# The up products of a SwiGLU block, re-formed as two nested levels of a seven-product scheme, on one Trainium2 core

## The chip, the cores and the metric

The kernel runs on one core of one Trainium2 chip. The metric is the device time of one execution in microseconds (us). Before the change it is 1042.5 us, the median of three runs (1040.97 to 1045.37). The core's engines have separate instruction queues: TensorE (PE) with its weight loads (PEld), VectorE (DVE), ScalarE (ACT), GpSimd (POOL) and SyncE (SP). DMA transfers are issued mainly by SP, the stores of one stage by ACT.

## The reference

Everything is float32. Eight batches of eight heads (576 positions of 64 values) go through a retention layer; its output, 4608 tokens of 512 values, goes through a SwiGLU block with 1536 hidden columns.

```python
scores = (1 / sqrt(64)) * q @ k.transpose(0, 1, 3, 2)
ret = scores * Dmat            # gamma_h ** (i - j) for i >= j, else 0
attn = ret @ v                 # (8, 8, 576, 64)
x = attn.transpose(0, 2, 1, 3).reshape(4608, 512)
g = x @ w_gate                 # (512, 1536)
silu = g * (1.0 / (1.0 + exp(-g)))
out = (silu * (x @ w_val)) @ w_out      # (1536, 512)
```

## The kernel before

**Stages.** The tokens are cut into a first tile of 512 and four tiles of 1024 (`n` = 1 to 4). Stage 0 makes the first tile with plain products, while the weights are being unpacked. Each later tile has an *up stage* (hidden values) and then a *down stage* (outputs). The retention layer is done in *ticks*, one for each batch and pair of heads: small matmuls on PE and pieces of work on DVE and ACT that are dealt out between the products (`part_on`). Each tick also loads the q, k and v of a later pair; this *head load* is 12 or 13 small DMAs on SP's queue (`load`, L306 to L317) and follows the transposes of the tick on DVE (L516), whose buffer it fills again. `merge` spreads ticks evenly over the products of a stage. Ticks stand in the up stages of tiles 1 and 2, in the down stages of tiles 1 and 2, and a few that have no load any more stand in tile 3.

**The up products before.** An up stage has three parts (`qd`), each giving 512 hidden columns of gate and of value. In one part the weights are 4 column blocks of 128 by 2 halves of the 512 inputs, and the tokens are 4 blocks of 256. The table `UP` writes out a scheme of 26 products for this, in place of the usual 32. A product has four matmuls (gate and value, two slices of 128 inputs; L1124), each with 128x128 weights and 256 columns. The line of a product in `UP` says which of four PSUM banks it adds to, which sum of x blocks it reads (made on DVE and POOL, L910), which sum of weight blocks (made on POOL in tile 1, L910 and L1095), and how the bank is then read: copies on ACT (L1058), sums with the bank on DVE (L1061), sums without it on POOL, and at last SiLU on ACT (L1145) and the gate-times-value product on DVE or POOL (L1148 to L1152).

**Weight operands.** In tile 1 the weights are in SBUF. Each operand (a block or a sum) is stored to DRAM once it has been used (`up_ops`, L1128, from ACT's queue, 256 KB). In tiles 2 to 4 the operands come back by DMA on SP's queue (`fetch`, L1022) to a ring of eight places: when product m is done, the fetch for product m + 8 is issued. The down stage uses the same ring (384 KB each). For the first down stage, eight fetches are issued in the last steps of tile 1's up stage. The order on each queue is the order of the program; nothing is reordered.

**After a product.** A bank is taken by the product whose line begins it and may be taken again once its last read is done. The list `rested` keeps the four banks in the order of their use.

Of the kernel before, what the change touches and what calls it, by code (L numbers as in the profile page):

```python
# [22 lines left out]
def tables(gamma, scale, L):  # L23
# [27 lines left out]
UP = [  # L51
    "0= | 8: sub 8 2 6, sub 9 0 8, sub 10 4 9 | 8: neg 8 6, sub 9 2 6, sub 10 3 7, add 11 1 10 | copy 0, copy 1",
    "1= | 10: sub 11 3 8, sub 12 7 11 | 3: nad 12 3 6 | copy 2, copy 3",
    "2= | 0:  | 9:  | copy 4, copy 5",
    "3= | 12:  | 11: sub 8 11 6 | copy 6",
    "0+ | 9:  | 12: add 9 2 3 | sub 2 b 2, sub 4 4 2, out 4 4",
    "1= | 4: sub 13 0 2 | 10: nad 11 11 0 | add 2 b 2, neg 12 2",
    "3+ | 11: add 14 4 12 | 8:  | add 1 b 1",
    "0+ | 13: sub 15 14 0 | 9: add 12 4 5, add 10 2 12, nad 8 7 10 | sub 5 5 b, out 6 5",
    "1+ | 14: sub 16 0 1, add 17 5 16 | 11:  | add 6 b 6",  # L60
    "3= | 15: sub 18 4 6, sub 19 5 18 | 0: add 6 6 7 | add 7 b 6, neg 0 7",
    "2+ | 17:  | 8: sub 9 3 0 | copy 4",
    "0= | 19: add 20 7 10 | 5: add 11 0 2 | copy 5",
    "1= | 6:  | 6: add 7 7 5 | sub 0 b 0, out 14 0",
    "3+ | 20: sub 21 4 17 | 9: add 8 5 6 | sub 3 b 3",
    "2= | 3: sub 22 16 6 | 11: add 0 0 1 | add 7 b 3, out 7 7",
    "0+ | 21: add 18 18 7 | 7: nad 9 1 3 | add 2 b 2, sub 4 4 2, add 5 5 4",
    "1+ | 22:  | 8: sub 11 1 10 | add 2 b 2, neg 13 2",
    "3= | 18: sub 23 1 3, sub 24 5 23 | 0: nad 6 6 12 | add 6 b 6",
    "0= | 7:  | 9: add 2 2 4 | add 1 b 1, add 3 b 3, neg 15 1, neg 3 3, add 6 6 3, neg 2 6",  # L70
    "2+ | 24: sub 1 1 5 | 11: sub 12 0 12 | add 3 b 3",
    "1+ | 16:  | 6:  | sub 4 b 4",
    "3= | 1: sub 2 16 2 | 2: sub 1 5 1 | sub 5 b 5, add 0 b 4, out 8 5, out 9 0",
    "2+ | 23: sub 25 7 24 | 12: nad 3 3 10 | add 7 b 4, out 1 7",
    "1+ | 2:  | 4:  | neg 10 b",
    "3+ | 25:  | 1:  | sub 3 b 3, out 11 3",
    "0= | 5:  | 3:  | add 4 b 4, neg 5 4",
]
# [55 lines left out]
]  # L134

# [20 lines left out]
def kernel(  # L156
# [739 lines left out]

    up, down = lines(UP), lines(DOWN)
    N = len(up)
# [13 lines left out]
    up_ops = [[dr.tile([P, 512], F32, name=f"up{qd}_{i}") for i in range(N)] for qd in range(NQ)]  # L912
# [85 lines left out]
    def up_view(qd):  # L998
        return lambda s: (w_up[:, qd, :, s // 2, s % 2, :] if s < 8
                          else extra[:, s - 8].rearrange("p (g x) -> p g x", g=2))  # L1000

    def x_view(n):
        return lambda s: (xs[n][:, 2 * (s // 4) : 2 * (s // 4) + 2, (s % 4) * TB : (s % 4 + 1) * TB] if s < 8
                          else xsum[s - 8].rearrange("p (c x) -> p c x", c=2))

# [4 lines left out]

    fetches = [("dn", 1, i) for i in range(N)]
    for n in range(2, NTILE):
        fetches += [("up", qd, i) for qd in range(NQ) for i in range(N)] + [("dn", n, i) for i in range(N)]
    fetched = [0]
    turn = [5, 4, 1, 6, 7, 2, 0, 3]

    def fetch():
        m = fetched[0]
        if m < len(fetches):
            what, a, i = fetches[m]  # L1020
            src = up_ops[a][i] if what == "up" else dn_ops[i]
            nc.sync.dma_start(out=ring[:, turn[m % 8], 0 : src.shape[-1]], in_=src)  # L1022
            fetched[0] += 1

    used = [0]

    def operand():
        m = used[0]
        used[0] += 1
        return ring[:, turn[m % 8]]  # L1030
# [15 lines left out]
    products = []  # L1046

    def reads(ops, bank, busy, result, spread=False):

        at = lambda a: bank if a == "b" else part[int(a)]  # L1050
        old = len(products)
        for op in ops:
            if op[0] in ("copy", "add", "sub"):
                while any(a == op[1] for a, _ in products):
                    products.pop(0)[1]()
                    old -= 1
            if op[0] == "copy":
                nc.scalar.copy(out=at(op[1]), in_=bank)  # L1058
            elif op[0] in ("add", "sub"):
                eng = nc.vector if "b" in op or (busy and not spread) else nc.gpsimd  # L1060
                eng.tensor_tensor(out=at(op[1]), in0=at(op[2]), in1=at(op[3]),  # L1061
                                  op=ALU.add if op[0] == "add" else ALU.subtract)
            else:
                product = result(int(op[1]), at(op[2]), op[0] == "neg", op[2] == "b" or busy)
                if product and op[2] == "b":
                    product()
                elif product:
                    products.append((op[2], product))
        for _ in range(old):
            products.pop(0)[1]()  # L1070


    x_ops = [op for line in up for op in line[3]]
    X_FIRST = 8

    def x_sums(n, lo, hi, vector):
        for op in x_ops[lo:hi]:
            add(nc.vector if vector or op[0] == "nad" else nc.gpsimd, op, x_view(n))

    def negated(qd, i):  # L1080

        view = up_view(qd)
        for op in up[i][5]:
            if op[0] == "nad":
                nc.scalar.mul(out=view(int(op[1])), in_=view(int(op[3] if op[3] == op[1] else op[2])), mul=-1.0)

    def w_sums(qd, i):
        view = up_view(qd)
        for op in up[i][5]:
            if op[0] == "nad":  # L1090

                dst, a, b = [view(int(s)) for s in op[1:]]
                if op[3] == op[1]:
                    a, b = b, a
                nc.gpsimd.tensor_tensor(out=dst, in0=dst, in1=b, op=ALU.subtract)  # L1095
            else:
                add(nc.gpsimd, op, view)

    def first_sums(qd, lo, hi):

        engines = [nc.scalar, nc.gpsimd, nc.vector, nc.gpsimd]
        for op, eng in list(zip(up[0][5], engines, strict=True))[lo:hi]:
            if op[0] == "neg":
                nc.scalar.mul(out=up_view(qd)(int(op[1])), in_=up_view(qd)(int(op[2])), mul=-1.0)
            else:
                add(eng, op, up_view(qd))

    def up_step(n, qd, i):
        label, opens, xslot, _, wslot, _, ops = up[i]
        busy = n == 1  # L1110
        if qd == 0:
            done = lambda i: X_FIRST + (min(3 * i, 2 * i + 2, i + 6) if busy else i)
            x_sums(n, done(i), done(i + 1), busy)
        if busy:
            if i > 1:
                w_sums(qd, i)
            w = up_view(qd)(wslot)
        else:
            w = operand()[:, 0:512].rearrange("p (g x) -> p g x", g=2)
        rhs = x_view(n)(xslot)  # L1120
        b = bank(label, i == 0)
        for gv in range(2):
            for c in range(2):
                m = nc.tensor.matmul(b[:, gv * TB : (gv + 1) * TB], w[:, gv, ts(c, P)], rhs[:, c, :],  # L1124
                                     start=(opens and gv == 0 and c == 0), stop=(c == 1), skip_group_check=True)
        stepped.append(m)
        if busy:
            nc.scalar.dma_start(out=up_ops[qd][i].rearrange("p (g x) -> p g x", g=2), in_=w)  # L1128
            if i in (20, 23) and qd + 1 < NQ:
                first_sums(qd + 1, *((0, 2) if i == 20 else (2, 4)))  # L1130
            if i == 24 and qd + 1 < NQ:
                negated(qd + 1, 1)
                w_sums(qd + 1, 1)
            if 0 < i < N - 1:
                negated(qd, i + 1)
            if qd + 1 == NQ:
                for _ in range({21: 3, 22: 2, N - 1: 3}.get(i, 0)):
                    fetch()
        else:
            fetch()  # L1140

        def result(o, src, negative, vector):
            s = io[:, (silus[0] % 4) * TB : (silus[0] % 4 + 1) * TB]
            silus[0] += 1
            nc.scalar.activation(out=s, in_=src[:, 0:TB], func=AF.Silu, scale=-1.0 if negative else 1.0)  # L1145
            dst = hid[:, qd, o // 4, o % 4]
            if negative:
                return lambda: nc.vector.scalar_tensor_tensor(out=dst, in0=src[:, TB : 2 * TB], scalar=-1.0, in1=s,  # L1148
                                                              op0=ALU.mult, op1=ALU.mult)
            if vector:  # L1150
                return lambda: nc.vector.tensor_tensor(out=dst, in0=src[:, TB : 2 * TB], in1=s, op=ALU.mult)
# [115 lines left out]
    for m, f in enumerate(down_order):  # L1267
# [5 lines left out]
        if m == 5:  # L1273
            first_sums(0, 0, 1)
# [71 lines left out]
```

## Time and profile before

| what | value |
|---|---|
| median of 3 runs | 1042.5 us |
| span of the profiled execution, first to last instruction | 1037.2 us |
| PE busy / PEld busy | 1023.1 us (99%) / 846.0 us (82%) |
| DVE / ACT / POOL busy | 633.2 (61%) / 299.6 (29%) / 419.9 us (40%) |
| up stage of tile 1 | 173.8 to 320.5 us |
| down stage of tile 1 | 320.5 to 400.3 us |
| up stages of tiles 2, 3, 4 | 400.3 to 545.5, 622.6 to 762.2, 831.4 to 966.0 us |
| DVE busy in the up stage of tile 1 / 2 / 3 / 4 | 105.1 / 76.1 / 68.0 / 56.9 us |
| POOL busy in the same | 96.6 / 49.7 / 51.4 / 49.6 us |

The page gives no separate time for the profiled execution; its span is 5.3 us below the median of the timed runs. Busy times say how much an engine had to do, not whether anybody waited for it. Waits are in the view of waits (who waited for whom) and in the view of instructions in order of time, which gives the start, the duration and, in square brackets, the idle time before an instruction and what ended it. [...]

### The profile page before, as it was taken

What the parts mean: (1) busy time and instruction counts of PE and PEld (TensorE: products, weight loads), DVE (VectorE), ACT (ScalarE), POOL (GpSimd) and SP (SyncE); (2) the same over time, 40 slices, a digit from 0 to 9 for tenths busy, and PEclk for the clock granted to TensorE, in tenths of its full rate; (3) what the DMA queues carried; (4) which work ended last, traced back from release to release, by engine and by line L of the source; (5) the groups of instructions that cost most, each with busy time, mean ns of one, the idle gap of its engine ahead of it and who ended that gap; (6) DMA issues with size and microseconds to landing.
All of it is one profiled execution on the core that took longest, in us unless ns stands there. A gap on an engine that the chain in (4) does not pass through costs nothing.

```text
span 1037.2 us, 21564 instructions
## 1 busy us (share of the span) xinstructions
PE 1023.1 (99%) x8440; PEld 846.0 (82%) x8440; DVE 633.2 (61%) x1070; ACT 299.6 (29%) x653; POOL 419.9 (40%) x369
## 2 busy tenths in 40 slices
PE   6999999999999999999999999999999999999998
PEld 5654555888888888888888888888888888888887
DVE  4488878676768667446458685435465644344644
ACT  3566433253544222222322103223211022231110
POOL 3401265867564236522134057222242583222425
PEclk9999999999999999999999999999999999999999
DMA  9999877777679887674686686555554465555653
GB/s 240 258 279 263 200 218 269 204 205 191 196 194 265 211 244 220 177 197 133 188 231 173 176 208 208 153 142 153 159 171 148 143 196 153 153 153 160 182 163 100
DMA packets 307244, 199.12 MB, mean 192 GB/s; under 512 B 215944, under 2 KB 251784, under 8 KB 307144
## 3 DMA queue, kind: packets, MB, share of 16 engines
q1 hardware_dynamic: 275720, 161.17, 58.2%
q10 hardware_dynamic: 30784, 36.18, 10.4%
q8 instruction: 67, 1.10, 0.5%
q0 software_dynamic: 640, 0.39, 0.2%
q14 instruction: 33, 0.27, 0.1%
HBM read 157.58 MB, written 40.11 MB: 191 GB/s over the span
## 4 chain that ended last, share of the span: by engine, by line
PE 93%; DMA 3%; DVE 1%; ACT 1%; issue 1%; SPq 1%; POOL 0%; DVEq 0%; ACTq 0%; POOLq 0%
PE bankC L1124 13%; PE bankE L1124 13%; PE bankB L1124 13%; PE bankA L1124 13%; PE bankB L1173 7%; PE bankC L1173 7%; PE bankE L1173 7%; PE bankA L1173 7%; PE outer L556 2%; PE bankA L877 2%; PE bankB L877 1%; PE bankE L877 1%; PE outer L583 1%; PE inner L597 1%; PE inner L567 1%; PE bankC L877 1%
## 5 line engine op out<-in xcount | busy, mean ns | idle before, releaser
L1061 POOL TENSOR_TENSOR rest<-rest 128x512 f32<-128x512 f32 x65 | 91.7, 1415 | 234.3 <-DVE rest L1061 212.8
L1145 ACT ACTIVATE io<-rest 128x256 f32<-128x256 f32 x180 | 75.0, 416 | 305.4 <-DVE rest L1061 262.4
L1124 PE MATMUL bankC<-rest,arena 128*128 128x256 f32 x544 | 129.0, 380 | 0.0
L1124 PE MATMUL bankA<-rest,arena 128*128 128x256 f32 x544 | 128.7, 379 | 0.0
L910 POOL TENSOR_TENSOR arena<-arena 128x512 f32<-128x512 f32 (+1 forms) x72 | 110.6, 1549 | 37.3 <-DMA up<-arena 26.5
L1124 PE MATMUL bankB<-rest,arena 128*128 128x256 f32 x512 | 121.2, 380 | 0.5 <-DMA arena<-up 0.5
L1124 PE MATMUL bankE<-rest,arena 128*128 128x256 f32 x512 | 121.4, 380 | 0.1
L1152 POOL TENSOR_TENSOR arena<-rest,io 128x256 f32<-128x256 f32 x72 | 51.9, 726 | 167.7 <-ACT io L1145 167.7
L1124 PEld LDWEIGHTS bankA<-rest,arena 128*128 128x128 f32 x544 | 103.2, 190 | 14.5 <-issue 0.5
L1124 PEld LDWEIGHTS bankC<-rest,arena 128*128 128x128 f32 x544 | 102.9, 190 | 14.4 <-POOL arena L910 0.3
L1124 PEld LDWEIGHTS bankB<-rest,arena 128*128 128x128 f32 x512 | 97.0, 190 | 14.0 <-issue 0.8
L1124 PEld LDWEIGHTS bankE<-rest,arena 128*128 128x128 f32 x512 | 97.0, 190 | 13.7 <-DVE rest L1061 0.5
L910 POOL TENSOR_TENSOR rest<-rest 128x256 f32<-128x256 f32 (+1 forms) x69 | 68.9, 1020 | 71.8 <-DMA dn<-rest 35.3
L1061 DVE TENSOR_TENSOR rest<-bankB,rest 128x512 f32<-128x512 f32 x72 | 48.9, 687 | 67.1 <-PE bankB L1124 52.5
L1061 DVE TENSOR_TENSOR rest<-bankC,rest 128x512 f32<-128x512 f32 x72 | 48.9, 687 | 65.5 <-PE bankC L1124 46.9
L1061 DVE TENSOR_TENSOR rest<-bankA,rest 128x512 f32<-128x512 f32 x72 | 48.9, 687 | 61.2 <-PE bankA L1124 45.1
L1061 DVE TENSOR_TENSOR rest<-bankE,rest 128x512 f32<-128x512 f32 x71 | 48.2, 687 | 60.5 <-PE bankE L1124 47.1
L1148 DVE SCALAR_TENSOR_TENSOR arena<-rest,io 128x256 f32<-128x256 f32 x84 | 56.7, 676 | 10.8 <-ACT io L1145 10.8
L1173 PE MATMUL bankC<-arena 128*128 128x256 f32 x252 | 58.3, 380 | 0.1
L1173 PE MATMUL bankB<-arena 128*128 128x256 f32 x252 | 58.2, 381 | 0.0
L1173 PE MATMUL bankA<-arena 128*128 128x256 f32 x252 | 57.9, 379 | 0.0
L1173 PE MATMUL bankE<-arena 128*128 128x256 f32 x252 | 57.9, 379 | 0.0
(204 smaller groups left out, 1626.1 us busy)
## 6 DMA issues: line engine op xcount, KB each, us to landing
arena<-up SPq DMA_DIRECT2D x234, 256.0 KB, 2.6
arena<-dn SPq DMA_DIRECT2D x104, 384.0 KB, 3.8
up<-arena ACTq DMA_DIRECT2D x78, 256.0 KB, 3.7
dn<-rest SPq DMA_DIRECT2D x78, 128.0 KB, 1.8
out_dram<-rest SPq DMA_DIRECT2D x31, 256.0 KB, 3.9
qk<-in_q_dram SPq DMA_DIRECT2D x108, 72.0 KB, 2.6
qk<-in_k_dram SPq DMA_DIRECT2D x108, 72.0 KB, 2.7
rest<-in_moe_w_out_dram ACTq DMA_DIRECT2D x6, 1024.0 KB
```

Of the source, the lines that this page charges most:

```text
L556: m = nc.tensor.matmul(value(i, hl, c), s["v"][rows, at], ret[rows, c % 2 if whole(i) else hl, c // 2], start=start, stop=start, skip_grou ...
L567: nc.tensor.matmul(z[half[hl], r, c], s["kn"][chunk(i, hl, 2 * c + r)], s["v"][rows, at], start=True, stop=True, skip_group_check=True)
L583: nc.tensor.matmul(xr[half[hl]] if c + 1 == NC else value(i, hl, c), state[half[hl], c, :], s["qT"][half[hl], ts(c, L)], start=False, stop ...
L597: nc.tensor.matmul(sc[chunk(i, hl, 2 * c + r)[0], r if whole(i) else hl, c], kT[half[hl], at], qT[half[hl], at], start=True, stop=True, sk ...
L877: nc.tensor.matmul(bank, w, xs[0][:, c, :], start=(c == 0), stop=(c == HP - 1))
L910: eng.tensor_tensor(out=dst, in0=srcs[0], in1=srcs[1], op=ALU.add if op[0] == "add" else ALU.subtract)
L1061: eng.tensor_tensor(out=at(op[1]), in0=at(op[2]), in1=at(op[3]), op=ALU.add if op[0] == "add" else ALU.subtract)
L1124: m = nc.tensor.matmul(b[:, gv * TB : (gv + 1) * TB], w[:, gv, ts(c, P)], rhs[:, c, :], start=(opens and gv == 0 and c == 0), stop=(c == 1 ...
L1145: nc.scalar.activation(out=s, in_=src[:, 0:TB], func=AF.Silu, scale=-1.0 if negative else 1.0)
L1148: return lambda: nc.vector.scalar_tensor_tensor(out=dst, in0=src[:, TB : 2 * TB], scalar=-1.0, in1=s, op0=ALU.mult, op1=ALU.mult)
L1152: nc.gpsimd.tensor_tensor(out=dst, in0=src[:, TB : 2 * TB], in1=s, op=ALU.mult)
L1173: nc.tensor.matmul(b[:, m * TB : (m + 1) * TB], lhs[:, qd, ts(m, P)], w[:, qd], start=(opens and qd == 0 and m == 0), stop=(qd == NQ - 1), ...
```

## The change

`UP`, `up_step` and the helpers for its sums go, with the sums that were made during stage 0's down products. In their place stands a seven-product scheme for 2 x 2 by 2 x 2 blocks. The outer level works on the halves of tokens, inputs and columns and gives seven products (here *sets*) for each part, in the order 1, 2, 6, 7, 4, 5, 3. In tile 1 each set is multiplied plainly (`PLAIN`): 8 *slots* of two matmuls. In tiles 2 to 4 all sets but the first two of a tile, `(0, 1)` and `(0, 2)`, are split again by the same scheme into seven slots of two matmuls; those two stay plain. A slot has one 128x128 block of weights for gate and one for value, and 256 columns.

The weights of a set are stored and fetched as one piece: 7 blocks for gate and 7 for value, 896 KB (512 KB for a plain set). The ring of eight places becomes three places of 1792 columns in the same memory for the up stages. The fetch of a set is issued when the set that held its place is finished. The sums of weights are made on POOL in tile 1, in two buffers of 1024 columns that lie in the memory which the down stage's first fetches fill; each buffer is stored from ACT's queue. The eight fetches for the first down stage are issued at the end of tile 1's up stage, after its last slot. In tiles 2 to 4 the order of slots overlaps neighbouring sets: 1, the old set's 7, then 5, 2, 6, the old set's 4, then 3. Within a set, one bank takes products 1, 6, 7 and 4 in turn, a second 5 and 3, a third 2, and each is read after each product. The last tile gets two more banks, in the tiles `inner` and `outer`. Ticks advance by a piece every second slot in tile 1 and every third in the others.

```diff
-UP = [
-    "0= | 8: sub 8 2 6, sub 9 0 8, sub 10 4 9 | 8: neg 8 6, sub 9 2 6, sub 10 3 7, add 11 1 10 | copy 0, copy 1",
...
+SETS = (1, 2, 6, 7, 4, 5, 3)
+PLAIN = {1: {(qd, o) for qd in range(3) for o in SETS}, 2: {(0, 1), (0, 2)}, 3: {(0, 1), (0, 2)}, 4: {(0, 1), (0, 2)}}
...
-    fetches = [("dn", 1, i) for i in range(N)]
-    for n in range(2, NTILE):
-        fetches += [("up", qd, i) for qd in range(NQ) for i in range(N)] + [("dn", n, i) for i in range(N)]
+    fetches = []
+    for n in range(1, NTILE):
+        for m, (qd, o) in enumerate([(qd, o) for qd in range(NQ) for o in SETS] if n > 1 else []):
+            fetches.append(("plain" if (qd, o) in PLAIN[n] else "fine", qd, o, m % 3 * 1792, 1024 if (qd, o) in PLAIN[n] else 1792))
+        turn = [5, 6, 7, 0, 1, 2, 3, 4] * 3 + [5, 6] if n == 1 else list(range(8)) * 3 + [4, 5]
+        fetches += [("dn", n, i, 768 * turn[i], 768) for i in range(N)]
...
     def fetch():
+        while fetched[0] < len(fetches):
+            lo, width = fetches[fetched[0]][3:]
+            if any(f[3] < lo + width and lo < f[3] + f[4] for f in fetches[used[0] : fetched[0]]):
+                return
+            fetch_one()
...
+    def w_sets(qd):
...
+        flat = arena[:, 4 * QW :]
+        new = [flat[:, 1024 * i : 1024 * (i + 1)].rearrange("p (g j x) -> p g j x", g=2, j=4) for i in range(2)]
...
+        def done(k):
+            if not busy:
+                used[0] += 1
+                fetch()
...
+        def whole_read(k, c, bank, at):
+            o = seq[k][1]
+            if o == 1:
+                nc.scalar.copy(out=to(k, c), in_=bank)
+            elif o == 5:
+                combine(nc.vector, held[c], bank, held[c], 1)
+                combine(nc.vector, to(k, c), bank, kept(k, c), 1)
+            else:
+                combine(nc.vector, to(k, c), bank, addend(k, c), 1)
+            made(k, c, at)
+
+        def first_read(k, c, bank):
+            qd, o = seq[k]
+            dst = to(k, c)
+            if o == 1:
+                nc.scalar.copy(out=dst, in_=bank)
+            elif o == 5 and c != 12:
+                nc.scalar.copy(out=dst, in_=bank)
+                combine(nc.gpsimd, held[c], held[c], dst, 1)
+                combine(nc.gpsimd, dst, dst, kept(k, c), 1)
+            elif o == 5:
+                combine(nc.vector, held[c], bank, held[c], 1)
+                combine(nc.vector, dst, bank, kept(k, c), 1)
+            elif qd > 0 and o != 3 and c != 12:
+                t = ends[0 if o == 4 else 1][c]
+                nc.scalar.copy(out=t, in_=bank)
+                combine(nc.gpsimd, dst, t, addend(k, c), 1)
+            else:
+                combine(nc.vector, dst, bank, addend(k, c), 1)
+
+        def second_read(k, c, bank, at):
+            if seq[k][1] == 5:
+                combine(nc.vector, held[c], bank, held[c], 1)
+            combine(nc.vector, to(k, c), bank, to(k, c), 1)
+            made(k, c, at)
...
+            if plain[k]:
+                own = [(k, c, half) for c in corners for half in range(2)]
+                own[2:2], own[6:6] = old[:1], old[1:]
+            else:
+                own = [(k, i) for i in (1, 5, 2, 6, 3)]
+                own[1:1], own[5:5] = old[:1], old[1:]
...
+                for i, o in enumerate(order):
+                    for j, f in enumerate(w_inner(o)):
+                        later(at + 8 + (13 * i + 3 * j) // 2, f)
+                    later(at + 8 + (13 * i + 9) // 2 + 6, *store(o, True))
...
+            if at % (2 if busy else 3) == 1:
+                part_on()
+            if at + 1 == len(slots):
+                while waiting:
+                    finish(*waiting.pop(0)[1:])
+                for t in sorted(after):
+                    for f in after[t]:
+                        f()
...
+                if busy:
+                    for _ in range(8):
+                        fetch_one()
```

## The prediction

> **What bounds the kernel now.** I read the page's busy rows and chain first, then the groups by line, the waits, and the instructions in order of time around the up stages.
>
> ```profile
> PE 1023.1 (99%) x8440; PEld 846.0 (82%) x8440; DVE 633.2 (61%) x1070; ACT 299.6 (29%) x653; POOL 419.9 (40%) x369
> ...
> PE 93%; DMA 3%; DVE 1%; ACT 1%; issue 1%; SPq 1%; POOL 0%; DVEq 0%; ACTq 0%; POOLq 0%
> ...
> L1124 PE MATMUL bankB<-rest,arena 128*128 128x256 f32 x512 | 121.2, 380 | 0.5 <-DMA arena<-up 0.5
> ```
>
> PE never stands still: in all four up stages its whole idle time is about half a microsecond. So a matmul saved is time saved at PE's pace, and any new wait of PE is lost in full. The pace is in PE's instructions at the start of tile 1's up stage:
>
> ```profile
> 173.84 1.89 PE L1124 MATMUL bankA<-rest,arena 128*128 128x256 f32 x8
> 175.57 1.89 PE L1124 MATMUL bankB<-rest,arena 128*128 128x256 f32 x8
> 177.29 1.89 PE L1124 MATMUL bankC<-x_odd,arena 128*128 128x256 f32 x8
> ```
>
> Starts are 1.727 us apart for eight records, that is four matmuls: 0.432 us for one.
>
> The one wait of 0.5 us is worth more than its size. It is in tile 2; first SP's queue there, then PE:
>
> ```profile
> 414.91 1.96 SPq L306 DMA_DIRECT2D qk<-in_q_dram  x4
> 416.91 3.08 SPq L306 DMA_DIRECT2D qk<-in_k_dram  x4
> 420.09 0.99 SPq L314 DMA_DIRECT2D kn<-in_k_dram  x2
> 421.12 1.06 SPq L314 DMA_DIRECT2D v<-in_v_dram  x2
> 422.22 0.54 SPq L317 DMA_DIRECT2D v<-in_v_dram  x1
> 422.86 8.15 SPq L1022 DMA_DIRECT2D arena<-up  x10
> ```
>
> ```profile
> 426.97 1.97 PE L1124 MATMUL bankB<-rest,arena 128*128 128x256 f32 x8 [0.46 <-DMA arena<-up]
> ```
>
> A head load held SP from 414.9 to 422.8. A weight fetch due at about 414.4 went out at 422.86, 8.4 late, and landed 3.97 later (the chain has it as "422.86 3.97 DMA arena<-up"). The ring of eight gave it seven products of lead, 7 x 1.727 = 12.1. 8.4 + 4.0 - 12.1 = 0.3, and PE waited 0.46. The change shortens that lead.
>
> **The change, term by term** (span of the profiled execution 1037.2; the runs' median 1042.5 is 5.3 above, which I carry over unchanged).
>
> *Matmuls, -7.8.* Before, 3 x 104 = 312 a tile, 1248. After, the built order has 336 in tile 1 (3 x 7 x 16) and 298 in tiles 2, 3 and 4 (19 x 14 + 2 x 16), 1230. 18 fewer x 0.432 = 7.8: tile 1 pays 10.4, the others gain 6.0 each. Shapes are the same, so is the pace. A slot (two matmuls) takes 0.864, a split set of seven 6.04.
>
> *Head loads in tile 2, +18 (13 to 24).* A set's fetch goes out when the set three before it is finished, in the sixth slot of the period after that one. From there to its use are 8 slots, 6.9, in place of 12.1. One fetch is 896 KB. In tile 4, where nothing else disturbs, the DMA view has
>
> ```profile
> arena<-up SPq DMA_DIRECT2D x72, 256.0 KB, 2.7
> arena<-dn SPq DMA_DIRECT2D x26, 384.0 KB, 3.2
> ```
>
> so 128 KB more cost about 0.45, and I estimate 2.7 + 5 x 0.45 = 4.95: on time by 1.9 alone. But the program puts four head loads into this stage, at slots 19, 55, 94 and 130, each between two fetches. A load starts when DVE has done the second transpose, about 2.8 slots after that (slot 1, read of the bank 0.69, transpose 0.76). In the trace it holds SP for 6.9 to 7.9; I take 7.2, 8.3 slots. So the next fetches go out at slots 30.1, 66.1, 105.1 and 141.1. They were due at 27, 62, 97 and 132: late by 2.7, 3.6, 7.0 and 7.9 us. Behind a load a fetch lands as the 3.97 above: 3.97 + 2.25 = 6.2. Lateness + 6.2 - 6.9 gives stalls of 2.0, 2.9, 6.3 and 7.2, together 18.4. With 4.95 they are 13.3; with 0.75 for each 128 KB (between the 0.45 and the page's medians, 2.6 and 3.8) they are 24.4. Tiles 3 and 4 have no head load.
>
> [...]
>
> *End of tile 1's up stage, +11 (8 to 14).* The first down fetch fills memory in which the last weight sums lie. Their store stands on ACT's queue behind the last SiLU, and the fetch behind the store; the built order shows that the fetch waits for the store's DMA. From PE's last matmul: bank read and SiLU, 0.2 + 0.69 + 0.42, with about 0.5 of DVE lag, 1.8; issue 0.35; 512 KB out, 3.7 (page, 256 KB `up<-arena`) + 0.9 = 4.6; issue and 384 KB in, 0.5 + 3.5: 10.8. PE's next instruction needs it and nothing is before it on the queue. The low end takes the 2.2 of tile 4's output stores (256 KB) for the 3.7, and 3.1 in, 8. The high end has DVE 3 late and the slower slopes, 14. Before, five of the eight fetches were issued up to five products earlier, and PE passes from L1124 to L1173 without a gap.
>
> *Bank reads, +3 (0 to 9).* DVE's read of a bank takes 0.69 alone and 0.61 in a row (in order of time, two take 1.29). Set 5 has ten of them and two copies, 6.1 in 6.04 of PE; also four POOL sums at 1.30 to 1.42 each. Its neighbours have five to seven reads. A bank is needed again three slots, 2.6, after its last product, so the lag of one set 5 is absorbed. Three of the nine meet retention pieces on DVE (two in tile 2, one in tile 3), and I charge 1 each. The upper end is 1 for all nine; a gain is excluded, because PE has no such wait to lose. Sums of x (POOL 0.82 each, four a set) are made a set ahead. In tile 1 DVE has 84 reads, 48 products at 0.70, 8 x sums at 1.04 and some 28 of retention, 128 in 157: covered, because there the slack is six slots.
>
> *Clock, +5 (0 to 9).* The granted clock falls well below 1 in one spell near the start, after a gap of 1.59 on a sparse PE. In the view by stretches (columns: us, then busy time of PE, PEld, DVE, ACT, POOL, then the granted clock):
>
> ```profile
> 15.00:20.00 5.00, 3.24 (x115) 2.80 (x116) 3.48 (x9) 1.08 (x3) 2.38 (x3) 0.84 1.18 279
> 20.00:25.00 5.00, 4.29 (x122) 3.50 (x114) 3.44 (x8) 3.34 (x8) 1.96 (x2) 0.81 0.89 248
> ```
>
> That is 0.16 x 5 + 0.19 x 5 = 1.75 lost for one such spell. I charge it for the three gaps above 6 us; none is the low end, all five gaps the high end.
>
> [...]
>
> *Costed at nothing:* the old sums that went (POOL 110 and DVE's x sums) were beside a PE that didn't wait for them. Stores from ACT's queue are as many bytes in 63 DMAs in place of 78.
>
> Sum: -7.8 + 18.4 + 11 + 3 + 5 = +30, so 1072. All low ends give +13, 1056; all high ends +49, 1091.
>
> **Rivals.**
> 1. *The loads are hidden*, because SP gets through them earlier than I place them or landing is faster: about 5 in place of 18, and no gap long enough for the clock but one: -7.8 + 5 + 11 + 3 + 2 = +13 at most, +5 with only 5 of the boundary and no clock: 1047 to 1055. Against it is the 8.4 of lateness in the trace. 0.10.
> 2. *Not slower: the lead suffices*, at the place where tile 2's fetches pass the head loads on SP. If a load holds SP so that a fetch is less than 1.9 late (6.9 - 4.95), PE doesn't wait; if the store at tile 1's end lands while PE still works as well, only the matmuls are left: 1035. With one of the two, within 0.5%. Against it: the load alone is 7 long. Faster 0.05, same 0.06.
> 3. *Every set waits for its fetch.* With the page's medians, 1.2 for each 128 KB, a set lands in 8.7 and comes 1.8 late, some 50 times: +92, 1165. The threshold is 0.84 for each 128 KB. Tile 4's two rows speak against it. 0.05.
> 4. *DVE and POOL bound the split sets*, by waiting for each other at each set 5: 2.5 x 9 = 22 in place of 3, 1091. 0.04.
>
> **Numbers.** The forecast has 0.70. 0.5% is about what a measurement of this kernel can tell from no change, here 5.2 us. Slower: forecast, rivals 1, 3 and 4, 0.89; same 0.06; faster 0.05. The range of 1046 to 1093 takes in the forecast's ends and rivals 1 and 4, and leaves out 2 and 3, with the edges of the forecast.
>
> **What would show it.** PE's matmuls number 18 fewer at the same pace. In tile 2, four idle times of PE ended by "DMA arena<-up", each after a head load on SP, two of them above 5 us. One gap of about 11 at the first down product of tile 1, ended by "DMA arena<-dn", and a clock below 1 just behind the long gaps. Tile 4's up stage 128.7 + at most 2, against 134.6. I am wrong if tile 2's fetches go out ahead of the loads, if PE waits for DVE or POOL more than for DMA, or if tiles 3 and 4 wait at every set.

## The result, and the profile after

The changed kernel takes 1088.9 us (median of four runs, 1085.9 to 1092.3); the kernel before, on the same chip, 1042.3 (1041.0 to 1045.4). The ratio is 1.0446, 95% interval 1.0413 to 1.048. The forecast was 1072, its range 1046 to 1093: the sign and the mechanism are right, and 17 us of cost are missing from the sum. The profiled execution has a span of 1088.6, 51.4 above that of before; the medians differ by 46.6. The profiled execution of the changed kernel was 1.4 above its median (1090.3), and by the remaining 3.4 before's was below its own.

The page's busy row, the chain by engine and the first PE group of the up stages, as they were shown of before:

```profile
PE 1030.4 (95%) x8404; PEld 844.7 (78%) x8404; DVE 685.0 (63%) x1177; ACT 288.5 (27%) x638; POOL 527.0 (48%) x567
...
PE 6%; DVE 0%; DVEq 0%; issue 0%
...
L1148 PE MATMUL bankB<-rest,arena 128*128 128x256 f32 x428 | 111.6, 388 | 5.9 <-DMA arena<-up 3.4
```

PE has 36 records fewer, two for each of the 18 matmuls saved, and is busy 7 us *longer*: twelve records are counted as 5.46 at a clock of 0.50, and the twelve behind them as 2.82 (below). The chain could be followed back through 6% of the span only, so it says nothing here. The waits do (what waited and for whom; total, times, longest, in us):

```profile
PE bankA L1309 <- DMA arena<-dn: 11.5, 1, 11.5
PE bankC L1148 <- DMA arena<-up: 6.3, 1, 6.3
PE bankA L1148 <- DMA arena<-up: 6.2, 1, 6.2
PE bankE L1309 <- DMA arena<-dn: 5.2, 1, 5.2
...
PE bankB L1148 <- DMA arena<-up: 3.4, 1, 3.4
PE bankB L1148 <- DVE rest L1037: 3.2, 4, 1.0
PE inner L573 <- issue: 2.8, 2, 1.5
```

Few waits for transfers, each of one piece: PE waits for six transfers (for the sixth, in tile 2's up stage, 0.6 only), and nothing waits at every set. The times between the first products of the stages say where they are:

| stage | before | after | difference |
|---|---|---|---|
| first tile and loading | 173.8 | 177.5 | +3.7 |
| tile 1 up, to its last matmul | 146.7 | 158.2 | +11.5 |
| gap behind it | 0 | 11.5 | +11.5 |
| tile 1 down | 79.8 | 82.2 | +2.5 |
| tile 2 up | 145.2 | 167.6 | +22.4 |
| tile 2 down | 77.1 | 85.3 | +8.2 |
| tile 3 up / down | 139.6 / 69.2 | 135.8 / 69.2 | -3.8 / 0 |
| tile 4 up / down | 134.7 / 67.5 | 130.0 / 67.5 | -4.7 / 0 |

**Tile 2's up stage.** SP's queue around the third head load, then PE (start, duration, and in brackets the idle time before):

```profile
528.77 1.96 SPq L282 DMA_DIRECT2D qk<-in_q_dram  x4
...
535.14 0.57 SPq L293 DMA_DIRECT2D v<-in_v_dram  x1
535.81 1.19 SPq L996 DMA_DIRECT2D arena<-up  x2
```

```profile
541.34 2.05 PE L1148 MATMUL bankA<-rest,arena 128*128 128x256 f32 x4 [6.19 <-DMA arena<-up]
```

It is the wait of before once more, larger: a load holds SP for 6.9 us (528.8 to 535.7), two fetches go out right behind it, and PE stands until the first has landed. Four matmul records then take 2.05 in place of 1.03.

**End of tile 1's up stage.** ACT, SP and PE in order of time:

```profile
338.84 0.42 ACT L1162 ACTIVATE io<-rest 128x256 f32<-128x256 f32 x1 [1.53 <-DVE rest L1037]
340.79 0.42 ACT L1162 ACTIVATE io<-rest 128x256 f32<-128x256 f32 x1 [1.53 <-DVE rest L1037]
340.87 0.52 ACTq L1094 DMA_DIRECT2D up<-arena  x1
```

```profile
338.18 0.55 SPq L287 DMA_DIRECT2D v<-in_v_dram  x1
343.99 3.94 SPq L993 DMA_DIRECT2D arena<-dn  x8
```

```profile
347.16 5.46 PE L1309 MATMUL bankA<-arena 128*128 128x256 f32 x12 [11.48 <-DMA arena<-dn]
352.41 2.82 PE L1309 MATMUL bankB<-arena 128*128 128x256 f32 x12
```

The last SiLU, the store, the fetch and the product follow each other as forecast. The first product takes 5.46, the second 2.82. The view by stretches has the reason (us, busy time of PE, PEld, DVE, ACT, POOL, then the granted clock):

```profile
347.00:350.00 3.00, 2.84 (x7) 2.33 (x8) 0.00 (x0) 0.00 (x0) 0.00 (x0) 0.50 0.92 280
350.00:353.00 3.00, 3.00 (x10) 2.41 (x9) 0.00 (x0) 0.34 (x1) 0.00 (x0) 0.58 1.04 408
353.00:356.00 3.00, 3.00 (x67) 2.46 (x69) 0.00 (x0) 0.83 (x2) 0.00 (x0) 1.00 0.77 281
```

**Tile 2's down stage**, which the forecast leaves out. SP, then PE:

```profile
663.24 1.97 SPq L282 DMA_DIRECT2D qk<-in_q_dram  x4
...
669.61 0.54 SPq L293 DMA_DIRECT2D v<-in_v_dram  x1
670.26 0.40 SPq L993 DMA_DIRECT2D arena<-dn  x1
```

```profile
658.83 2.75 PE L1309 MATMUL bankC<-arena 128*128 128x256 f32 x12
...
666.60 2.75 PE L1309 MATMUL bankC<-arena 128*128 128x256 f32 x12
674.61 5.46 PE L1309 MATMUL bankE<-arena 128*128 128x256 f32 x12 [5.25 <-DMA arena<-dn]
```

A head load stands ahead of a late fetch here too. The list `turn` in the diff ends in `[4, 5]`: the last operand takes the place of the one four products earlier, so its fetch has the three products between them as lead, 7.8 us. It was due when the product of 658.83 was done, at 661.6. But the load stands ahead of it on SP, first waiting for its transposes on DVE until 663.24 and then issuing for 7.0, and the fetch went out at 670.26, 8.7 late. It took 4.35 to the product: 8.7 + 4.35 - 7.8 = 5.25, the wait.

### The profile page after: what moved, and what is told of

It reads as the page before. It is cut to its first block, busy times and chain, and to the rows that moved or that the text cites. A ratio compares the mean times of both kernels' runs of the same rounds, so it can differ in the third digit from the quotient of the medians.

```text
span 1088.6 us, 21367 instructions
## 1 busy us (share of the span) xinstructions
PE 1030.4 (95%) x8404; PEld 844.7 (78%) x8404; DVE 685.0 (63%) x1177; ACT 288.5 (27%) x638; POOL 527.0 (48%) x567
## 5 line engine op out<-in xcount | busy, mean ns | idle before, releaser
L1037 POOL TENSOR_TENSOR rest<-rest 128x512 f32<-128x512 f32 (+1 forms) x136 | 141.9, 1053 | 228.3 <-DVE rest L1037 169.2
L1163 POOL TENSOR_TENSOR arena<-rest,io 128x256 f32<-128x256 f32 x144 | 105.1, 740 | 51.1 <-ACT io L1162 50.8
L1037 POOL TENSOR_TENSOR arena<-arena 128x256 f32<-128x256 f32 (+1 forms) x108 | 94.7, 904 | 69.1 <-DMA up<-arena 47.5
L1037 DVE TENSOR_TENSOR rest<-bankA,rest 128x512 f32<-128x512 f32 x93 | 63.1, 687 | 69.2 <-PE bankA L1148 30.1
L1148 PE MATMUL bankA<-rest,arena 128*128 128x256 f32 x388 | 99.7, 385 | 6.2 <-DMA arena<-up 6.2
L1148 PEld LDWEIGHTS bankB<-rest,arena 128*128 128x128 f32 x428 | 82.1, 194 | 19.5 <-DVE rest L1037 4.4
L1148 PE MATMUL bankE<-rest,arena 128*128 128x256 f32 x352 | 89.1, 382 | 1.5 <-DVE rest L1037 0.8
L1148 PEld LDWEIGHTS bankA<-rest,arena 128*128 128x128 f32 x388 | 74.4, 193 | 17.3 <-issue 6.6
L1148 PEld LDWEIGHTS bankE<-rest,arena 128*128 128x128 f32 x352 | 67.0, 191 | 12.3 <-DVE rest L1037 1.3
L886 POOL TENSOR_TENSOR rest<-rest 128x256 f32<-128x256 f32 x43 | 34.4, 822 | 71.9 <-DVE rest L407 37.8
L1309 PE MATMUL bankA<-arena 128*128 128x256 f32 x240 | 57.9, 393 | 11.5 <-DMA arena<-dn 11.5
L1309 PEld LDWEIGHTS bankA<-arena 128*128 128x128 f32 x240 | 47.1, 197 | 18.7 <-issue 11.8
L1309 PEld LDWEIGHTS bankC<-arena 128*128 128x128 f32 x288 | 54.5, 190 | 7.5
```

The source lines that it names most:

```text
L886: eng.tensor_tensor(out=dst, in0=srcs[0], in1=srcs[1], op=ALU.add if op[0] == "add" else ALU.subtract)
L1037: eng.tensor_tensor(out=out, in0=a, in1=b, op=ALU.add if sign > 0 else ALU.subtract)
L1148: m = nc.tensor.matmul(b[:, g * TB : (g + 1) * TB], w[:, g], x, start=(opens and g == 0), stop=True, skip_group_check=True)
L1163: (nc.vector if busy else nc.gpsimd).tensor_tensor(out=hid[:, qd, 2 * H + h, 2 * T + t], in0=src[:, TB : 2 * TB], in1=s, op=ALU.mult)
L1309: nc.tensor.matmul(b[:, m * TB : (m + 1) * TB], lhs[:, qd, ts(m, P)], w[:, qd], start=(opens and qd == 0 and m == 0), stop=(qd == NQ - 1), ...
```

## The experiments

Each kernel was timed against the kernel before on its own chip. That one's median moved between 1038.6 and 1042.8 from chip to chip, so ratios are compared.

| kernel | before, same chip | median | ratio, 95% interval |
|---|---|---|---|
| changed | 1042.3 | 1088.9 | 1.0446 (1.0413 to 1.048) |
| tile 2's loads behind fetches | 1038.6 | 1061.8 | 1.0221 (1.0186 to 1.0255) |
| last store early | 1038.6 | 1080.4 | 1.0403 (1.0362 to 1.0444) |
| 24 idle products | 1038.6 | 1088.5 | 1.047 (1.0435 to 1.0505) |
| 29 idle products | 1039.9 | 1084.8 | 1.0426 (1.0394 to 1.0457) |
| load 31 behind a fetch | 1038.6 | 1080.2 | 1.0394 (1.0356 to 1.0432) |
| all orders | 1039.9 | 1044.2 | 1.004 (1.0017 to 1.0063) |
| and the last set's order | 1039.9 | 1044.3 | 1.0033 (1.0012 to 1.0053) |
| and later sums | 1040.7 | 1040.3 | 1.0005 (0.9986 to 1.0025) |
| and load 20 later | 1042.8 | 1044.1 | 1.0017 (0.9999 to 1.0035) |

### Head loads of tile 2 behind the next fetch

```diff
-        tick(t, FIRST, NP, True, lambda: next_load(t))
+        tick(t, FIRST, NP, True, lambda: late.append(t) if t + AHEAD in (24, 25, 26, 27) else next_load(t))
...
                 fetch()
+                while late:
+                    next_load(late.pop(0))
```

The second edit is in `done`, so a held load goes out after the next set's fetch.

> Only the order on SP changes: each of the four head loads in tile 2's up stage is issued just after the next fetch of a set instead of before it. Same transfers, same bytes, same matmuls. If the four waits of PE there (0.6, 3.4, 6.2 and 6.3 us) come from the order on SP, a fetch is now at most 1.1 us late and lands in 5.0, inside its lead of 6.9: all four waits fall below 0.5 us, and with them the slow matmuls behind the gaps (about 7 us). Tile 2's up stage goes from 167.6 to about 144 us, the time from 1089 to about 1066. If the rival holds, that fetches of 896 KB land late beside a head load because the DMA engines are full, waits of some us stay at the same four places and the time gains less than 8.

The median fell by about 2.2% of the kernel before, 23 us. Tile 2's up stage takes 145.4 in place of 167.6. What is left of its waits for weights:

```profile
PE bankB L1149 <- DMA arena<-up: 2.3, 1, 2.3
...
PE bankA L1149 <- DMA arena<-up: 1.5, 1, 1.5
```

The expectation had all four below 0.5; two are not. The transfers are as large as before, and only their order on SP is changed, so the order is the cause of this part. A load behind a fetch held SP longer here, 8.8 to 10.0 us in place of 6.9 to 8.3, and the two waits that are left stand at fetches that went out right behind such a load. 12.7 us less of waiting took 22.2 off the stage: with it went about 6.6 of lowered clock and a wait of 1.5 with the releaser "issue"; the last 1.4 is not assigned. Rival 3 (sets too large to land in time) falls.

### The last store of tile 1's up stage early

```diff
-                    later(at + 8 + (13 * i + 9) // 2 + 6, *store(o, True))
+                    later(at + 8 + (13 * i + 9) // 2 + (2 if (qd, i) == (2, 6) else 6), *store(o, True))
```

> Only the last store of weight sums in tile 1 is issued from ACT's queue before the last SiLUs instead of behind them. If the first down fetch waits for this store, the store goes out about 5.7 us earlier, and the wait of 11.5 us shrinks until the next thing holds SP, the head load that ends 3.2 us after PE's last matmul: to about 6.3, the time to about 1083 to 1084. If SP's head load or the landing of the fetch itself were the limit already, the wait stays at 11 to 11.5 and the time is unchanged.

The wait went from 11.5 to 8.1, where 6.3 was expected, and the ratio from 1.0446 to 1.0403; the intervals overlap, so the size rests on the profile. The store no longer waits for the last SiLU (it is issued at 329.47, six us ahead of that SiLU's 335.51). SP now shows what is late next:

```profile
332.67 1.12 SPq L287 DMA_DIRECT2D v<-in_v_dram  x1
333.93 4.59 SPq L993 DMA_DIRECT2D arena<-dn  x8
```

The fetches go out as head load 19 ends. Two chains end at this fetch, the store on ACT and the load on SP, a few us apart; taking away one gives only the distance to the other.

### Idle products in the gap, 24 and 29

```diff
                     for _ in range(8):
                         fetch_one()
+                    for _ in range(24):
+                        nc.tensor.matmul(banks[rested[0]][:, 0:TB], xs[1][:, 0, 0:P], xs[1][:, 1, 0:TB],
+                                         start=True, stop=True, skip_group_check=True)
```

Their results are never read. The second kernel has 29 in place of 24.

> 24 matmuls whose results nobody uses are added between tile 1's last up slot and its first down product, 10.4 us of work inside the gap of 11.5. Nothing else changes. If the slow matmuls behind the gap (the first twelve take 5.2 us in place of 2.6) come from PE having stood still, they run at 2.6 and the time falls by about 2.7 us although PE has more to do. If they are slow because of what goes on beside them (transfers that land then), they stay slow and the time is the same.

> [...] Theory A (the clock falls after a pause, however short, and the 24 left a pause of 1.9 us): the first product takes about 2.75 us in place of 5.46, at full clock; the time is 2 to 2.5 us less than the changed kernel's. Rival B (the clock falls at a stage's start for another cause, the load's traffic or the change of operands): the first product is slow again, and the time that of the run with 24.

With 24, PE had 1.90 us of idle time left, and that was enough:

```profile
334.56 10.52 PE L1296 MATMUL bankA<-x_odd 128*128 128x256 f32 x48
346.98 4.51 PE L1312 MATMUL bankA<-arena 128*128 128x256 f32 x12 [1.90 <-DMA arena<-dn]
351.33 2.75 PE L1312 MATMUL bankB<-arena 128*128 128x256 f32 x12
```

With 29, no idle time:

```profile
332.78 12.68 PE L1296 MATMUL bankA<-x_odd 128*128 128x256 f32 x58
345.37 2.83 PE L1312 MATMUL bankA<-arena 128*128 128x256 f32 x12
```

The same product on the same operand takes 5.46 after 11.5 us of idle time, 4.51 after 1.9, 2.83 after none. So it is the pause, and neither the load's traffic nor the operands, that makes the product slow, by some 2.6 us here. In time the first kernel gained nothing (its up stage drew some 0.9 us more in other waits, and the first weights landed 0.8 later behind its last matmul), the second about 2 us, which the intervals don't separate from the changed kernel.

### Head load 31 behind the fetch in tile 2's down stage

As the first experiment's edit, with `t + AHEAD in (31,)`, and the two lines of `while late` behind `fetch()` in `down_step`.

> Only the last head load, in tile 2's down stage, is issued after the fetch of the last down operand and of the next tile's first two sets instead of before them. A wait of 5.25 us at the last down product of tile 2 and about 2.8 us of slow matmuls behind it were not in the forecast. If that wait is the same mechanism in another place (the fetch's lead is four products there, 10.4 us, and the head load takes 7), both go: about 8 us less, 1081. If the wait comes from the short lead alone, some 2 to 5 us of it stay.

The stage takes 77.14, as before the change, in place of 85.34, and the product that waited stands in line, at full pace (its fetch had a lead of three products, not the four of the expectation):

```profile
663.69 2.75 PE L1310 MATMUL bankC<-arena 128*128 128x256 f32 x12
666.28 1.89 PE L1310 MATMUL bankE<-arena 128*128 128x256 f32 x8
```

So 8.2 us hung on one load ahead of one fetch, 5.25 of waiting and 2.9 of clock. By the ratios it is 5.4 us (0.52%), each of them known to about 4.

### All orders

The first, second and fourth edits together, load 19 held as well, and three lines for tile 1's end:

```diff
-        turn = [5, 6, 7, 0, 1, 2, 3, 4] * 3 + [5, 6] if n == 1
+        turn = [0, 2, 6, 7, 5, 1, 3, 4] * 3 + [6, 7] if n == 1
...
+            if busy and at == 158:
+                fetch_one()
+                fetch_one()
...
-                    for _ in range(8):
+                    for _ in range(5):
                         fetch_one()
+                    while late:
+                        next_load(late.pop(0))
+                    fetch_one()
```

The first two down operands now go to places that are free while tile 1 is still at work.

> The changed kernel with every order repaired at once: head loads 24 to 27 and 31 behind the next fetch, the last weight sum of tile 1's up stage stored early, and at tile 1's boundary three of the stored sums taken late in the walk so that two fetches need not wait for the last store, with head load 19 behind five more fetches. Theory A (order on SP's queue and the store's chain are the whole cost): the waits for loads at the two down stages (11.5 and 5.25 us) and the three in tile 2 fall to at most 4 us together, their half-clock periods go, and what is left of the change is 7.8 us of matmuls saved against about 5.6 us of waits for bank reads and up to 4 of loads: 1038 to 1044, within 0.5% of the kernel before. Rival B (the loads themselves need the time: moving them only moves the waits): head loads now collide with the tick that needs them, and 1050 or more.

1.004: by the ratios 4 us above the kernel before and 42 below the changed one. No wait for "arena<-dn" is left, one of 0.6 for "arena<-up", and the mean granted clock is 0.998, as before. So the late transfers with the clock behind them are the loss, nearly all of it, and the order of issue makes them, at tile 1's end together with the places of the first operands. What is left of the new waits are reads by DVE, 4.7 us in all, and one of 2.35 with the releaser "issue".

### The last set's order

In a split tile's last set the closing slots 7 and 4 came behind slot 3; now:

```diff
+            if k + 1 == K and not plain[k]:
+                own = [(k, 1), old[0], (k, 5), (k, 6), old[1], (k, 2), (k, 7), (k, 3), (k, 4)]
             slots += own
-        if not plain[-1]:
-            slots += [(K - 1, 7), (K - 1, 4)]
```

> The kernel of the run before, with the slots of each split tile's last set in another order, so that the two that end the set do not follow each other on one bank's read. Theory A: the wait of about 1 us for VectorE's bank read at the end of the up stages of tiles 2, 3 and 4 goes, 2 to 3 us less than the run before. Rival: VectorE is late by its load, not by the order, and the wait comes back one slot later: no difference.

The wait of 1.03 went, but tiles 3 and 4 gained 0.46 and 0.45 only: three or four pauses of 0.1 to 0.3 stand in its place, since DVE is without a pause in those 6 us. Half order, half load. The time is the same. This profile has a larger thing, at 198 us in tile 1. ACT, then PE:

```profile
195.53 0.52 ACTq L1095 DMA_DIRECT2D up<-arena  x1
196.09 0.63 ACTq L1096 DMA_DIRECT2D up<-arena  x1
196.77 0.42 ACT L1165 ACTIVATE io<-rest 128x256 f32<-128x256 f32 x1 [8.61 <-POOL arena L1038]
```

```profile
198.48 3.78 PE L1149 MATMUL bankB<-x_odd,arena 128*128 128x256 f32 x8 [3.49 <-DVE rest L1038]
```

A SiLU stands behind stores that wait for POOL's weight sums; DVE's product waits for the SiLU (idle for 5.10 us, by the view), the bank reads wait behind that product, and PE for a bank. In eight profiles of kernels with the change this wait is between nothing and 3.5 us.

### Sums of tile 1's first part later

```diff
-                        later(at + 8 + (13 * i + 3 * j) // 2, f)
+                        later(at + (8 if qd else 12) + (13 * i + 3 * j) // 2, f)
```

The same for the store of these sums.

> The kernel with all orders repaired and the last set reordered, with the first part's inner weight sums in tile 1 and their stores 4 slots later. In the profile of the run before, a SiLU of the second set stands on ACT's queue behind two stores that wait for POOL's sums, VectorE's product waits for that SiLU, the bank reads wait behind the product, and PE waits 3.49 us at 198.5. Theory A (the place on ACT's queue decides): with the store behind that SiLU the wait goes in tile 1's first part, 0.4 to 3.5 us, about 1.5 on the median, so 1042 to 1043 where the kernel before has 1040. Rival B (POOL is late in any case): a later store delays the sums of the sets after it, and the wait returns later in the part; no difference or slower.

The wait at 198 is gone: the SiLU is done at 192.1, the store follows at 195.9. 1.0005: the kernel before and this one can't be told apart. Against the run before it the intervals overlap, so that this edit is worth time is shown by the profile alone. A new wait came in tile 1's down stage, on SP again:

```profile
365.14 0.70 SPq L293 DMA_DIRECT2D v<-in_v_dram  x1
365.96 2.27 SPq L994 DMA_DIRECT2D arena<-dn  x5
```

```profile
369.83 2.40 PE L1318 MATMUL bankA<-arena 128*128 128x256 f32 x10 [2.37 <-DMA arena<-dn]
```

### The next head load one product later

Load 20 joins the held ones, and in `down_step` the loop reads `while late and not (n == 1 and i == 3)`.

> The kernel of the last timed run, with the next head load of tile 1's down stage (load 20) issued one product later, so that the fetches of the twelfth and thirteenth down weights go out ahead of its 13 DMAs. In the profile of the run before, that load held SP from 353.2 to 365.8, the twelfth fetch went out at 365.96 and PE waited 2.37 us for it. Theory A (the order on SP again): the wait goes, the stage takes 79.7 us in place of 82.1, and the time falls by 1 to 2.4 us, to 1038 to 1039.5, 0.1 to 0.3% below the kernel before, which is within what a measurement can tell from no change. Rival B: the load now ends later and the fetch behind it, the fourteenth, is late in its turn: the same wait, one or two products on.

The stage takes 79.8 in place of 82.1 and has no such wait, so the order was the cause here as well. The time did not follow: 1.0017. The profiled execution lost more than the gain earlier: tile 1's up stage begins at 179.6 in place of 174.5 and takes 161.1 in place of 159.4. A wait of 2.1 with the releaser "issue" is in both, but here the two products behind it take 5.25 us to the start of the next one in place of 3.56, 1.7 lost.

### The kernel before, twice more

> The kernel before, unchanged, for one more profile. The first stage's code is the same in all kernels, but tile 1's up stage began at 173.8 us in the profile of before and between 172.0 and 178.3 in those of the changed kernels. If that is variation between executions, it will begin between 172 and 178 here too, and the 3.7 us by which the first stage of the changed kernel was longer are no cost of the change. If the change costs something there (code loading, for one), before stays within half a microsecond of 173.8.

> The same as the run ahead of it, a third profile of the kernel before: the start of tile 1's up stage between 172 and 178 if the first stage varies by itself, 173.8 within half a microsecond if it does not.

Tile 1 begins at 173.3 and 172.2 (spans 1036.1 and 1036.2). The first fits both expectations, the second only that of variation. So the first stage varies in the kernel before, by 1.7 us over three profiles. In the ten of kernels with the change it begins between 172.0 and 179.6, 175.0 on average against 173.1. Part of the 3.7 is variation; whether the change costs two us there, with its other code on all engines, stays open.

## Why the forecast was right in kind and 17 us short

Its terms, against the profile after:

| term | forecast | measured |
|---|---|---|
| Matmuls | -7.8 | -7.8 |
| Head loads in tile 2 | +18 | +16.5 |
| End of tile 1's up stage | +11 | +11.5 |
| Bank reads | +3 | +5.6 |
| Clock | +5 | about +12 |
| Tile 2's down stage | not in it | +5.25 |
| First stage; "issue" | not in it | +3.7; +1.2 |

That makes 48 of the 51.4; the rest is in pieces too small to assign. Against medians the forecast is 17 short; against these two profiles it is 21, because of the executions that they caught.

*Matmuls* is right: 36 records, the same 1.727 between starts. Tile 4's up stage, 128.7 plus at most 2 in the forecast, took 130.0.

*Head loads* is right, but for the first place: 2.0, 2.9, 6.3 and 7.2 were forecast, 0.6, 3.4, 6.2 and 6.3 came, and a set landed in 5.0 (median) where 4.95 was estimated:

```profile
arena<-up SPq DMA_DIRECT2D x57, 896.0 KB, 5.0
...
up<-arena ACTq DMA_DIRECT2D x21, 512.0 KB, 4.6
```

*End of tile 1's up stage* is right in size by luck, since its errors cancel. The last SiLU was done 5.5 after PE's last matmul (335.68), not 1.8, because DVE was late. There reads of a bank and gate-times-value products alternate, and the products are slow beside sums on POOL (a sum with the product beside it, then a product with no sum beside it):

```profile
336.00 1.87 POOL L886 TENSOR_TENSOR rest<-arena 128x768 f32<-128x768 f32 x1
336.72 1.42 DVE L1163 TENSOR_TENSOR arena<-rest,io 128x256 f32<-128x256 f32 x1
...
340.62 0.41 DVE L1163 TENSOR_TENSOR arena<-rest,io 128x256 f32<-128x256 f32 x1
```

Of the 48 such products in tile 1, 25 take longer than 0.5 us, and each of the 25 ends 0.28 after a POOL instruction that was running when it began; the others take about 0.41. Reads of a bank take 0.68 beside POOL too. So these products waited for POOL's sums, not for the SiLU, and DVE's last read began 4.3 after PE's last matmul, where the sum has 0.5 of lag and its high end 3. On the other side, the store took 3.1 from its issue to the fetch, where issue and landing were put at 4.95, and the fetch 3.2 to the product, not 4.0. The forecast also had one chain where there are two: the early store uncovered the head load.

*Bank reads* was right in the places that it charged, and left others out. "The lag of one set 5 is absorbed" held, apart from the three sets that the forecast charged because they meet retention pieces, two in tile 2 and one in tile 3. Those cost 0.7, 0.46 and 0.46 in place of 1 each. In the third, a transpose stands among DVE's reads, which follow each other without a pause:

```profile
766.45 0.77 DVE L492 STREAM_TRANSPOSE qT<-qk 128x576 f32<-128x576 f32 x1
```

```profile
768.45 1.13 PE L1148 MATMUL bankB<-rest,arena 128*128 128x256 f32 x4 [0.46 <-DVE rest L1037]
```

Left out were 1.05 in tile 1 and, in tiles 2 to 4, the end of the last set, where two slots follow each other on one bank, 0.85, 1.03 and 1.04:

```profile
1014.25 1.03 PE L1148 MATMUL bankB<-rest,arena 128*128 128x256 f32 x4
1016.32 1.13 PE L1148 MATMUL bankB<-rest,arena 128*128 128x256 f32 x4 [1.04 <-DVE rest L1037]
```

Starts are 2.07 apart in place of 0.86.

*Clock* is the term that fell short by the most: "1.75 lost for one such spell. I charge it for the three gaps above 6 us." The row was of a sparse PE near the start. Behind the gaps the clock is 0.50 for 2.8 to 5.8 us of dense work: 2.5 lost in tile 1's down stage (82.2 against the 79.8 with no gap), 2.9 in tile 2's (85.3 less the wait of 5.25 and the undisturbed 77.1), 1.4, 2.9 and 2.3 in tile 2's up stage (from the clock by stretches, 3.1 us at 0.54 for the first). And all five gaps above 3 us (3.39 to 11.48) had the lowered clock behind them, not only three. The kernel of 24 idle products has a clock by single us of 0.82, 0.50, 0.50, 0.50, 0.98 behind its pause of 1.90, 1.7 lost; this profile loses up to 2.9 behind one gap, where the row that the forecast charged has 1.75.

*Tile 2's down stage* is the step left out. Head loads were counted against the fetches of the up stages only, because there the ring was made shorter. But `turn` in the same diff gave one down fetch a lead of three products, and a load stands there too.

Of the rivals, the first (the loads are hidden) falls by the 16.5 of waits. "The lead suffices" needs lateness below 1.9, and it was more; with the loads moved it became true, and its price then was not 1035 but 1040 to 1044. Rival 4, which has PE wait for DVE and POOL at every set 5, falls by the waits for reads, 5.6 in all. The saving of matmuls is real: in the kernel with later sums tiles 2, 3 and 4 take 141.6, 135.3 and 129.5 for their up stages, 3.6, 4.2 and 5.2 less than before. But tile 1's takes 12.7 more, 10.4 of it the matmuls of one level in place of the old scheme. Had every wait gone, 7.8 would be left.

## What to carry to other kernels

Where a change makes transfers larger and their ring shorter, list every other instruction on the issuing queue, in the next stage too, and compare lead minus landing with the time that it holds the queue, including the time for which it waits there for its own input; what isn't urgent goes behind the fetch. Charge a long pause of PE twice, once for itself and once for the lowered clock behind it: in the changed kernel the pauses of 3.39 to 11.48 us cost 1.4 to 2.9 us each in this second way. At a stage's end follow every chain into the first instruction of the next one, since removing the last to arrive gains only the distance to the one before.

## What the runs showed that was not expected

The clock doesn't go by the length of a pause alone. Behind the pause of 1.49 us with tile 2's loads behind fetches the next slots start 0.94 and 0.86 apart (0.86 before it), and behind that of 2.37 with later sums the clock was 1.00 (371 to 373). Behind the 1.90 with 24 idle products it was 0.50 (348 to 351). Two pauses with the releaser "issue" are almost alike: behind the 2.05 with later sums the next products start 1.83 and 1.73 apart, behind the 2.12 with load 20 later 2.37 and 2.88. With 29 idle products PE was busy for 0.28 of the 3 us from 491 to 494, and the clock of the next 3 was 1.00; with load 31 behind a fetch it was busy for 0.17 of the 3 from 494 to 497, and the clock of the next 3 was 0.50. Behind the five pauses of 3.39 to 11.48 in the changed kernel it was 0.50 each time. What decides for the shorter ones the runs don't show.

In the view by single us of the changed kernel the clock was already lowered in the microsecond at whose end PE began to work again (499.92), and it rose in the one from 502:

```profile
499.00:500.00 1.00, 0.09 (x1) 0.12 (x1) 0.00 (x0) 0.00 (x0) 0.00 (x0) 0.66 0.92 330
...
502.00:503.00 1.00, 1.00 (x4) 0.79 (x4) 0.00 (x0) 0.90 (x2) 0.34 (x1) 0.63 0.00 0
```

The 13 small DMAs of a head load held SP for 6.9 us in the changed kernel where the last fetch had gone out 7 us ahead of them (528.8 to 535.7), and for 12.6 (353.2 to 365.8) right behind four down fetches in the kernel with later sums.

A wait of PE's small matmuls (L573) of 2.0 to 2.4 us, with the releaser "issue", came in tile 1's up stage at about 280 us in five of the ten profiles of kernels with the change (2.05 at 279.60 with later sums, 2.12 at 284.75 with load 20 later), and in none of the three of the kernel before. The view names no semaphore for it, and its cause stays open.
